# Order of row tiles in the combination of an attention kernel, and the queue of its first feature loads

## The chip, the cores and the metric

The program runs on one core of one Trainium2 chip. The metric is the device time of one execution in microseconds (us). The engines are TensorE (PE, matrix products; PEld is its weight load), VectorE (DVE), ScalarE (ACT), GpSimd (POOL) and SyncE (SP), which here only issues DMAs. Each engine works through its own instructions in the order of the program, and semaphores hold one back until the results that it needs are there.

## What is computed

The reference has two independent halves, laid side by side in the output. Half B is a two-dimensional Fourier transform, a product with a complex weight, and the inverse; the change doesn't touch it. Half A is attention with a memory, 32 heads of 18 columns, over 2048 rows in four groups of 512:

```python
for s in range(N):                       # N = 4 groups of L = 512 rows
    qs, ks, vs = q[:, :, s], k[:, :, s], v[:, :, s]
    p = softmax(qs @ ks.T * scale + mask)      # causal mask
    a_dot = p @ vs
    pq = phi(qs)                         # features
    a_mem = (pq @ M) / (pq . z + 1e-6)
    outs.append(g * a_mem + (1 - g) * a_dot)
    M = M + phi(ks).T @ vs;  z = z + sum(phi(ks))
return o @ wo
```

## The kernel before

The 576 columns of half A (32 heads x 18) lie on partitions, as five row tiles: t = 0 to 3 have 126 rows (seven heads), the fifth, t = 4, has 72, which the kernel lays out as 96 by repeating 24 rows (`host_wo`, `atables`). Products in 32 bits are split in a high and a low part, so that three products of parts stand for one.

`attention` (L959) is a loop of 133 steps t; step t treats one head of one group (32 steps to a group). In a step, `s1` finds the row maxima of the scores for the head ten steps ahead (PE L660 to L669, DVE L664 and L670), `s2` makes the scores again, transposed, and their exponentials (PE L703, L707, L712; ACT L704, L709, L713; causal selections on POOL), and `pv` mixes the values (PE L733). `mpath` (L678) brings the maxima of four heads into two rows of Q: casts on POOL (L685), a transposition on PE (L689), a copy on ACT and a small DMA on POOL's queue (L693). The loads of the stacks Q and K are put in a list `q` and issued by SP, two to a step.

Beside this run two kinds of other work. `lane` holds generators that are taken one piece further in each step. `bg` is a list of generators of which `run_bg` takes one piece at fixed places: in the middle and at the end of every second step, and now and then at the end of the others. So the order of everything on each engine is written out by the program; nothing is planned at run time. `later(1, f)` (L924) runs f at the end of the step in which it is called from `run_bg`. `s.now` is the number of the step that ended last.

The background work of group g, from its step 11 or so on:

- `ux_load` (L824) loads the unnormalized attention result of the group before, tile by tile, into three buffers. For t = 4 it is one DMA with a first dimension of 2 and a second of 48 rows (L829), for the others one of 126 rows (L826).
- `combine(g-1)` (L834) works through five tiles. For a tile, PE spreads the reciprocal denominators over rows (`pb`, L854), DVE multiplies (L859; L857 for the first group) and POOL or, from `now` = 117 on, DVE adds the memory's part (L860). Two tiles later ACT makes the high part `oh` (L848) and POOL or DVE the low part `ol` (L843). For t = 4, `tail` (L830) copies 32 rows of the high part into the last rows of `oh` and `ol`: on ACT, or on DVE when `now` is over 116.
- `mem1(g, t)` (L810) multiplies the features `pq` of a tile by the memory (PE L814), copies (ACT L816), spreads and multiplies by its denominators (PE L820, DVE L821). It also has the next group's features loaded (`pq_load`, L774).
- `oproj` (L879) is the output projection: four blocks of 128 rows in two halves; a half is 14 products of parts on PE (L891) with a pause after the seventh, and a copy on ACT (L893).
- `mixed(g)` (L864) strings these together by letters: c is a piece of `combine(g-1)`, m a piece of `mem1`, p a piece of `oproj(2)`, in the last group only. In the first groups `between` does the projection afterwards.

PSUM banks for `pb`, `pn` and `po` come from `bank` (L807): one buffer "post" while `now` < 119, then three buffers "s1" until 130, then "s2", which also holds the scores of `s2`. So until then a `pb` has to wait until the `pb` or `pn` before it has been read.

After step 132 a loop takes the rest of `bg` piece by piece. In its rounds 3, 5 and 7 stands `last_tile` (L896), which combines a tile of the fourth group (PE L901, DVE L902 and L903, ACT L904, DVE L909); then `last_proj` (L917) makes the last output products (L923).

The features of the second group, `pq_load(1, .)`, are loaded at steps 16 to 20 through SP's queue (L989).

Of the kernel before, what the change touches and what calls it, by code (L numbers as in the profile page):

```python
# [393 lines left out]
class ATT:  # L394
# [356 lines left out]
    def recip(s,src,dst,gate,eps,load,slack=0):  # L751
# [21 lines left out]
        yield  # L773
    def pq_load(s,g,t):  # L774

        r=126 if t<4 else 72
        x=s.tp.tile([126,512],F32,name="pq",bufs=5)
        s.nc.sync.dma_start(x[:r],s.pqD[g][126*t:126*t+r])
        s.pq[g,t]=x
# [19 lines left out]
    def between(s,g,lane):  # L799

        o=s.oproj(g-1)
        for _ in range(4):
            next(o)
            yield
        yield from s.den(g+1,lane)
        yield from o
    def bank(s,name,r=126):  # L807

        return (s.ps if s.now<119 or s.now>130 else s.ps1).tile([r,512],F32,name=name,tag="post" if s.now<119 else "s1" if s.now<131 else "s2")
    def mem1(s,g,t):  # L810
        nc=s.nc; r=126 if t<4 else 96; e=126 if t<4 else 72
        pn=s.bank("pn")
        M=s.Mst[g][:e,t,:r]
        nc.tensor.matmul(pn[:r],M,s.pq.pop((g,t))[:e],start=True,stop=True)  # L814
        am=s.tp.tile([126,512],F32,name="am",bufs=5)
        nc.scalar.copy(am[:r],pn[:r])  # L816
        if g<3: s.later(1,lambda: s.pq_load(g+1,t))
        yield
        pb=s.bank("pb")
        nc.tensor.matmul(pb[:r],s.sel[:,t,:r],s.rc["rd"],start=True,stop=True)  # L820
        nc.vector.tensor_tensor(am[:r],am[:r],pb[:r],op=OP.mult)  # L821
        s.am[t]=am; s.amg[t]=g
        yield
# [10 lines left out]
    def combine(s,g):  # L834
# [6 lines left out]
        def low(u):  # L841
            r=126 if u<4 else 96
            eng().tensor_tensor(s.ol[u][:r],s.am[u][:r],s.oh[u][:r].bitcast(F32),op=OP.subtract)  # L843
        for t in range(7):
            if t>1:
                u=t-2; r=126 if u<4 else 96
                s.oh[u]=tp.tile([128,512],F32R,name="oh",bufs=5); s.ol[u]=tp.tile([128,512],F32R,name="ol",bufs=5)
                nc.scalar.copy(s.oh[u][:r],s.am[u][:r])  # L848
                if u==4: s.later(1,lambda oh=s.oh[4],ol=s.ol[4]: s.tail(oh,ol)) if s.now<117 else s.tail(s.oh[4],s.ol[4])
                if s.now<117: low(u)  # L850
            if t<5:
                r=126 if t<4 else 96; x=xs[t]
                pb=s.bank("pb")
# [4 lines left out]
                else:  # L858
                    nc.vector.tensor_tensor(x[:r],x[:r],pb[:r],op=OP.mult)  # L859
                    eng().tensor_tensor(s.am[t][:r],x[:r],s.am[t][:r],op=OP.add)  # L860
                if t<2: s.later(1,lambda t=t: s.ux_load(g,t+3))
            if t>1 and s.now>=117: low(t-2)
            yield
    def mixed(s,g):  # L864

        c=s.combine(g-1); M=[s.mem1(g,u) for u in range(5)]
        P=s.oproj(2) if g==3 else None
        for x in "cccccm"+"cmmcmmcmmcmm"+"m" if g<3 else "c"*9+"p"*8+"mp"*8:
            if x=="c": next(c,None); yield
            elif x=="p": next(P); yield  # L870
            else:
                while M:
                    try: next(M[0]); break
                    except StopIteration: M.pop(0)
                yield
# [3 lines left out]
    def oproj(s,g):  # L879
        nc=s.nc  # L880
        oh,ol=s.oh,s.ol
        for tb in range(4):
            ob=s.tp.tile([128,576],F32,name="ob")
            c=slice(128*tb,128*tb+128)
            for hf in range(2):
                ps=s.bank("po",128)[:,:288]
                w=slice(288*hf,288*hf+288)
                L=[(a,b,t) for a,b in ((oh,s.woh),(oh,s.wol),(ol,s.woh)) for t in range(4)]+[(oh,s.woh,4),(ol,s.wol,4)]
                for i,(a,b,t) in enumerate(L):
# [69 lines left out]
    def attention(s,tp,ps):  # L959
# [20 lines left out]
        for t in range(133):  # L980
# [7 lines left out]
            st=t%32  # L988
            if 16<=t<21: s.pq_load(1,t-16)  # L989
            if t==34: bg.append(s.den(1,lane))  # L990
            if st==8 and g>0:
                def ln(g=g):
                    r=s.recip(s.rD[g-1],s.rrD[g-1],s.g1,False,"rr",2)
                    for i in range(8):
                        next(r)
                        if 2<i<6: s.ux_load(g-1,i-3)
                        yield
# [180 lines left out]
```

## Time and profile before

| | us |
|---|---|
| median of 3 runs | 720.09 (719.54 to 721.27) |
| profiled execution | 716.54 |
| its span, first to last instruction | 714.8 |
| ACT busy | 448.5 |
| POOL busy | 213.0 |
| DMA queue of SP, share of 16 engines' span | 50.9% |

The profile is of one execution. Its page gives busy times and a chain of waits; the trace behind it can be asked for single stretches: a timeline by engine (start, duration, engine, line, operation, and in brackets the idle time ahead of it and what ended that), the chain in order of time, waits by line, and tables of busy time, granted PE clock and DMA share in chosen windows. Times in it count from the span's start. The busy time of PE is modelled and overlaps from one product to the next, so that a product's length in a run of them is read from start to start.

### The profile page before, as it was taken

What the parts mean: (1) busy time and instruction counts of PE and PEld (TensorE: products, weight loads), DVE (VectorE), ACT (ScalarE), POOL (GpSimd) and SP (SyncE); (2) the same over time, 40 slices, a digit from 0 to 9 for tenths busy, and PEclk for the clock granted to TensorE, in tenths of its full rate; (3) what the DMA queues carried; (4) which work ended last, traced back from release to release, by engine and by line L of the source; (5) the groups of instructions that cost most, each with busy time, mean ns of one, the idle gap of its engine ahead of it and who ended that gap; (6) DMA issues with size and microseconds to landing.
All of it is one profiled execution on the core that took longest, in us unless ns stands there. A gap on an engine that the chain in (4) does not pass through costs nothing.

```text
span 714.8 us, 14142 instructions
## 1 busy us (share of the span) xinstructions
PE 674.9 (94%) x4835; PEld 494.8 (69%) x4835; DVE 554.4 (78%) x1231; ACT 448.5 (63%) x1006; POOL 213.0 (30%) x421
## 2 busy tenths in 40 slices
PE   4999999999999999999999899999999999997997
PEld 4999769879879779999844444444566445663676
DVE  6999989799799699787587778887667876577153
ACT  3667785575575564444487777777667676677631
POOL 2110000200200211465167433554233752336110
PEclk9999999999999999999999999999999999999999
DMA  9876436545373568899537665666656666441332
GB/s 343 266 233 204 149 123 199 184 157 185 136 232 127 165 208 270 213 230 233 169 108 183 170 170 145 176 165 167 152 126 178 163 167 152 101 137 45 99 93 77
DMA packets 83752, 121.56 MB, mean 170 GB/s; under 512 B 11498, under 2 KB 51032, under 8 KB 83544
## 3 DMA queue, kind: packets, MB, share of 16 engines
q1 hardware_dynamic: 77088, 104.62, 50.9%
q0 software_dynamic: 6592, 16.04, 8.1%
q8 instruction: 38, 0.62, 0.4%
q14 instruction: 34, 0.28, 0.1%
HBM read 82.30 MB, written 38.24 MB: 169 GB/s over the span
## 4 chain that ended last, share of the span: by engine, by line
PE 68%; DVE 14%; ACT 6%; DMA 5%; issue 5%; POOL 1%; SPq 0%; DVEq 0%; ACTq 0%; POOLq 0%
PE pv L733 10%; PE pjv L468 8%; PE pj L468 7%; PE po L891 6%; PE s L660 5%; PE i L300 4%; PE i L311 4%; PE s L668 4%; PE s L703 3%; DVE junk L664 3%; PE s L707 2%; PE po L923 2%; DVE pj L487 2%; PE c L163 2%; PE f L142 2%
## 5 line engine op out<-in xcount | busy, mean ns | idle before, releaser
L664 DVE CUSTOM_DVE_ANT_0 junk<-s,mask 128x512 bf16<-128x512 f32 (+1 forms) x256 | 141.6, 553 | 56.9 <-PE s L660 45.9
L670 DVE TENSOR_REDUCE mx<-s 128x4 f32<-128x512 f32 x128 | 87.9, 687 | 17.1 <-PE s L669 15.5
L704 ACT ACTIVATE P<-s 128x512 f32<-128x512 f32 x128 | 77.1, 602 | 21.1 <-PE s L703 18.5
L733 PE MATMUL pv<-P,vs 128*32 128x512 f32 (+3 forms) x1024 | 82.9, 443 | 0.0
L709 ACT ACTIVATE P<-s 128x512 f32<-128x512 f32 x128 | 77.0, 602 | 7.3 <-PE s L708 3.8
L713 ACT ACTIVATE P<-s 128x256 f32<-128x256 f32 x128 | 49.5, 387 | 49.6 <-PE s L712 49.6
L716 POOL TENSOR_SCALAR_AFFINE_SELECT P<-P 128x512 f32<-128x512 f32 x116 | 69.3, 635 | 4.9 <-ACT P L704 4.7
L733 PEld LDWEIGHTS pv<-P,vs 128*32 128x32 f32 x1024 | 27.0, 109 | 45.2 <-issue 43.1
L468 PE MATMUL pj<-x,wqkh 128*128 128x512 f32 x162 | 55.9, 406 | 0.0
L517 POOL MEMSET vt<- 128x32 f32 x16 | 2.4, 160 | 150.2 <-PE pm L527 122.8
L210 DVE TENSOR_TENSOR t<-Z 128x580 f32<-128x580 f32 x64 | 46.1, 755 | 0.1
L210 DVE TENSOR_TENSOR Z<-t 128x580 f32<-128x580 f32 x64 | 45.8, 755 | 0.1
L660 PE MATMUL s<-Ks,Qs 108*128 108x512 bf16 (+1 forms) x128 | 42.2, 329 | 0.0
L142 PE MATMUL f<-ftab,eh 128*128 128x290 f32 (+1 forms) x160 | 31.4, 315 | 9.5 <-DMA ftab<-ftab 9.5
L491 ACT CAST sp<-pj 128x512 bf16<-128x512 f32 x36 | 21.0, 585 | 30.0 <-DVE pj L487 30.0
L300 PE MATMUL i<-civ,Y 128*128 128x256 f32 (+1 forms) x288 | 37.9, 284 | 1.3 <-DVE T L332 1.3
L300 PEld LDWEIGHTS i<-civ,Y 128*128 128x128 f32 (+1 forms) x288 | 35.9, 181 | 1.6 <-DVE T L332 1.6
L311 PE MATMUL i<-itab,T 128*128 128x290 f32 (+1 forms) x224 | 36.1, 310 | 0.1
L468 PEld LDWEIGHTS pj<-x,wqkh 128*128 128x128 f32 x162 | 30.4, 188 | 7.7 <-issue 1.0
L468 PE MATMUL pj<-x,wqkl 128*128 128x512 f32 x90 | 35.5, 395 | 0.0
L468 PE MATMUL pj<-xh,wqkh 128*128 128x512 f32 x90 | 35.5, 395 | 0.0
L468 PE MATMUL pj<-xh,wqkl 128*128 128x512 f32 x90 | 35.5, 395 | 0.0
(226 smaller groups left out, 1836.4 us busy)
## 6 DMA issues: line engine op xcount, KB each, us to landing
qkD<-sp SPq DMA_DIRECT2D x36, 384.0 KB
Ks<-qkD SPq DMA_DIRECT2D x72, 144.0 KB
x<-qkD SPq DMA_DIRECT2D x60, 144.0 KB
Qs<-qkD SPq DMA_DIRECT2D x60, 144.0 KB
xin<-xb SPq DMA_DIRECT2D x16, 384.0 KB
cfw<-cfw POOLq DMA_DIRECT2D x16, 384.0 KB, 4.5
civ<-civ POOLq DMA_DIRECT2D x16, 384.0 KB, 7.4
vs<-vD SPq DMA_DIRECT2D x16, 330.0 KB
```

The costliest lines, as they stand in the source:

```text
L210: v.tensor_tensor(o,a,b,op=op)
L300: nc.tensor.matmul(p[:m,k],Y[i][:,q,c*128:c*128+m],cc[:,hl,o:o+256],start=n==0,stop=n==5)
L311: nc.tensor.matmul(p,x,t,start=n==0,stop=n==6)
L468: s.nc.tensor.matmul(out,a,b,start=i==0,stop=i==len(L)-1)
L660: nc.tensor.matmul(out,Q[:108,h,128*i:128*i+128],K[:108,h,:128*(i+1)],start=True,stop=True)
L664: nc.vector.tensor_tensor_reduce(out=junk[:,:w],in0=src,in1=s.mask[:,512-w:],scale=1.0,scalar=-3.0e38, op0=OP.add,op1=OP.max,accum_out=s.m ...
L670: nc.vector.tensor_reduce(out=s.mx[k][:,hh],in_=pa.rearrange("p (b c) -> p b c",c=128),axis=mybir.AxisListType.X,op=OP.max)
L704: nc.scalar.activation(P[0][:,hh],p0,AF.Exp,scale=SC)
L709: nc.scalar.activation(P[1][:,hh],p1,AF.Exp,scale=SC)
L713: nc.scalar.activation(P[2][:,hh],p2,AF.Exp,scale=SC)
L716: if k<29: nc.gpsimd.affine_select(out=x,in_=x,pattern=pat+[[1,128]],compare_op=OP.is_ge,fill=0.0,base=0,channel_multiplier=-1)
L733: nc.tensor.matmul(s.pvt[32*hh:32*hh+32,128*j:],vt[:,j,19*h:19*h+32],mv[0][:,hh,mv[1]],start=j==0,stop=j==2,skip_group_check=True)
```

## The change

Four things are changed. The fifth row tile comes first: `ORD=(4,0,1,2,3)` is the order of the loads of `ux` and of the features, of `combine`, and of `mem1` in the first groups; the features of the fourth group are loaded so that its `mem1` keeps the order 0 to 4. In `combine` of the third group the high and low parts of a tile come three tiles later instead of two (`lag`), so that it has one piece more, which `mixed(3)` places behind the first piece of `oproj(2)`. In `oproj` the 14 products of a half go tile by tile: tile 4's high product, the high and low weights' products of tiles 0 to 3, tile 4's low product, then the low parts of tiles 0 to 3. The first features are loaded through POOL's queue.

```diff
--- before.py
+++ after.py
@@ -771,11 +771,11 @@
         nc.sync.dma_start(r,dst)
         s.rc[load]=r
         yield
-    def pq_load(s,g,t):
+    def pq_load(s,g,t,eng=None):
 
         r=126 if t<4 else 72
         x=s.tp.tile([126,512],F32,name="pq",bufs=5)
-        s.nc.sync.dma_start(x[:r],s.pqD[g][126*t:126*t+r])
+        (eng or s.nc.sync).dma_start(x[:r],s.pqD[g][126*t:126*t+r])
         s.pq[g,t]=x
     def den(s,g,lane):
         nc=s.nc; tp=s.tp
@@ -804,6 +804,7 @@
             yield
         yield from s.den(g+1,lane)
         yield from o
+    ORD=(4,0,1,2,3)
     def bank(s,name,r=126):
 
         return (s.ps if s.now<119 or s.now>130 else s.ps1).tile([r,512],F32,name=name,tag="post" if s.now<119 else "s1" if s.now<131 else "s2")
@@ -814,7 +815,7 @@
         nc.tensor.matmul(pn[:r],M,s.pq.pop((g,t))[:e],start=True,stop=True)
         am=s.tp.tile([126,512],F32,name="am",bufs=5)
         nc.scalar.copy(am[:r],pn[:r])
-        if g<3: s.later(1,lambda: s.pq_load(g+1,t))
+        if g<3: s.later(1,lambda: s.pq_load(g+1,t if g<2 else s.ORD.index(t)))
         yield
         pb=s.bank("pb")
         nc.tensor.matmul(pb[:r],s.sel[:,t,:r],s.rc["rd"],start=True,stop=True)
@@ -841,15 +842,16 @@
         def low(u):
             r=126 if u<4 else 96
             eng().tensor_tensor(s.ol[u][:r],s.am[u][:r],s.oh[u][:r].bitcast(F32),op=OP.subtract)
-        for t in range(7):
-            if t>1:
-                u=t-2; r=126 if u<4 else 96
+        lag=2 if g<2 else 3
+        for p in range(5+lag):
+            if p>=lag:
+                u=s.ORD[p-lag]; r=126 if u<4 else 96
                 s.oh[u]=tp.tile([128,512],F32R,name="oh",bufs=5); s.ol[u]=tp.tile([128,512],F32R,name="ol",bufs=5)
                 nc.scalar.copy(s.oh[u][:r],s.am[u][:r])
                 if u==4: s.later(1,lambda oh=s.oh[4],ol=s.ol[4]: s.tail(oh,ol)) if s.now<117 else s.tail(s.oh[4],s.ol[4])
                 if s.now<117: low(u)
-            if t<5:
-                r=126 if t<4 else 96; x=xs[t]
+            if p<5:
+                t=s.ORD[p]; r=126 if t<4 else 96; x=xs[t]
                 pb=s.bank("pb")
                 nc.tensor.matmul(pb[:r],s.sel[:,t,:r],s.rc["rr"],start=True,stop=True)
                 if g==0:
@@ -858,14 +860,14 @@
                 else:
                     nc.vector.tensor_tensor(x[:r],x[:r],pb[:r],op=OP.mult)
                     eng().tensor_tensor(s.am[t][:r],x[:r],s.am[t][:r],op=OP.add)
-                if t<2: s.later(1,lambda t=t: s.ux_load(g,t+3))
-            if t>1 and s.now>=117: low(t-2)
+                if p<2: s.later(1,lambda p=p: s.ux_load(g,s.ORD[p+3]))
+            if p>=lag and s.now>=117: low(u)
             yield
     def mixed(s,g):
 
-        c=s.combine(g-1); M=[s.mem1(g,u) for u in range(5)]
+        c=s.combine(g-1); M=[s.mem1(g,u) for u in (s.ORD if g<3 else range(5))]
         P=s.oproj(2) if g==3 else None
-        for x in "cccccm"+"cmmcmmcmmcmm"+"m" if g<3 else "c"*9+"p"*8+"mp"*8:
+        for x in "cccccm"+"cmmcmmcmmcmm"+"m" if g<3 else "c"*9+"p"+"c"+"p"*7+"mp"*8:
             if x=="c": next(c,None); yield
             elif x=="p": next(P); yield
             else:
@@ -885,7 +887,7 @@
             for hf in range(2):
                 ps=s.bank("po",128)[:,:288]
                 w=slice(288*hf,288*hf+288)
-                L=[(a,b,t) for a,b in ((oh,s.woh),(oh,s.wol),(ol,s.woh)) for t in range(4)]+[(oh,s.woh,4),(ol,s.wol,4)]
+                L=[(oh,s.woh,4)]+[(oh,b,t) for t in range(4) for b in (s.woh,s.wol)]+[(ol,s.wol,4)]+[(ol,s.woh,t) for t in range(4)]
                 for i,(a,b,t) in enumerate(L):
                     r=126 if t<4 else 128
                     nc.tensor.matmul(ps,a[t][:r,c],b[:r,t,w],start=i==0,stop=i==13)
@@ -986,14 +988,14 @@
                 if 0<n<13: q+=s.stack_dmas(n+3,1)
                 if n+2<16: q.append(lambda n=n: s.load_v(n+2))
             st=t%32
-            if 16<=t<21: s.pq_load(1,t-16)
+            if 16<=t<21: s.pq_load(1,s.ORD[t-16],nc.gpsimd)
             if t==34: bg.append(s.den(1,lane))
             if st==8 and g>0:
                 def ln(g=g):
                     r=s.recip(s.rD[g-1],s.rrD[g-1],s.g1,False,"rr",2)
                     for i in range(8):
                         next(r)
-                        if 2<i<6: s.ux_load(g-1,i-3)
+                        if 2<i<6: s.ux_load(g-1,s.ORD[i-3])
                         yield
                     yield from r
                     bg.append(s.mixed(g))
```

## The prediction

> **What bounds the kernel now.** I read the busy shares first, then the chain of work that ended last, then the waits, and at last single stretches by engine. The page's first part gives the owner of the span:
>
> ```profile
> PE 674.9 (94%) x4835; PEld 494.8 (69%) x4835; DVE 554.4 (78%) x1231; ACT 448.5 (63%) x1006; POOL 213.0 (30%) x421
> ```
>
> TensorE (PE) is busy 94% of 714.8 us, and the change takes no matrix product away. So it can only win back PE's idle time, some 40 us in many pieces, at the few places that it touches. The largest such place is in the third group, where the chain of waits leaves PE:
>
> ```profile
> 650.52 6.94 DMA ux<-uD
> ...
> 657.55 0.70 DVE ux L859
> ...
> 658.26 0.70 DVE am L860
> ...
> 659.01 0.50 issue
> 659.51 0.59 ACT P L709
> ...
> 660.15 0.32 PE s L707
> ```
>
> Columns: start, duration, what. Row tile 4 is loaded last, with the two-part transfer of L829. It lands 6.94 us after its issue begins. VectorE (DVE) stands before its product L859 until then; ScalarE (ACT) stands before tile 4's high part with the exponential L709 queued behind; and PE needs the bank that L709 frees. The PE rows of that stretch, and the clock in stretches of 3.41 us (busy time of PE, PEld, DVE, ACT, POOL, then clock, DMA share, GB/s), show the price:
>
> ```profile
> 660.15 0.32 PE L707 MATMUL s<-x,Ks 110*128 110x384 bf16 x1 [2.02 <-ACT P L709]
> ...
> 665.82 0.39 PE L703 MATMUL s<-x,Ks 110*128 110x512 bf16 x1
> ```
> ```profile
> 8.73:12.14 3.41, 2.03 (x7) 1.55 (x7) 2.39 (x5) 0.83 (x1) 0.00 (x0) 1.00 1.14 390
> ...
> 657.26:660.67 3.41, 1.40 (x11) 0.78 (x15) 3.09 (x5) 1.98 (x5) 0.27 (x1) 1.00 0.03 10
> 660.67:664.08 3.41, 3.41 (x22) 1.77 (x15) 1.62 (x4) 1.64 (x4) 0.00 (x0) 0.50 0.00 0
> 708.46:711.87 3.41, 1.49 (x12) 1.25 (x10) 1.77 (x4) 1.45 (x4) 0.00 (x0) 1.00 0.58 220
> 711.87:714.80 2.93, 0.00 (x0) 0.00 (x0) 0.00 (x0) 0.00 (x0) 0.00 (x0) 0.50 0.41 147
> ```
>
> PE idles 2.02 us, and then runs 3.41 us at half clock, which costs 3.41 x 0.5 = 1.7 us more. Two stretches with about 2 us idle (3.41 - 1.40 and 3.41 - 1.49) are followed by half clock, and one with 1.38 us idle (3.41 - 2.03) isn't. From 665.82 on, PE has a backlog of output products until the tail.
>
> **The change, part by part.** Times are of the profiled execution (716.54 us, of which 714.8 are its span); I carry the difference over to the median of the runs shown, 720.09, which lies 3.55 above it.
>
> *First features by GpSimd's queue.* These rows are SP's queue, GpSimd (POOL) and PE around steps 16 to 22:
>
> ```profile
> 391.08 1.98 SPq L644 DMA_DIRECT2D Qs<-qkD  x2
> ```
> ```profile
> 390.46 1.41 POOL L629 TENSOR_TENSOR woh<-woh,wol 128x576 fp32r<-128x576 f32 x1
> 392.10 0.20 POOL L685 CAST mh<-mg 128x16 bf16<-128x16 f32 x1 [0.23 <-PE s L703]
> ...
> 394.73 0.67 POOL L693 DMA_DIRECT2D x<-mts  x1
> ```
> ```profile
> 393.29 0.32 PE L668 MATMUL s<-Ks,x 108*128 108x384 bf16 x1 [0.39 <-DVE mg L664]
> ```
> ```profile
> 401.23 0.38 PE L668 MATMUL s<-x,Qs 108*128 108x384 bf16 x2 [1.02 <-DMA pq<-pqD]
> ```
> ```profile
> SPq L644 <- DMA pq<-pqD: 7.2, 8, 1.4
> ```
>
> Five loads leave SP's queue, three of them ahead of the last pieces of the Qs stack, issued from 391.08 on, which the product at 401.23 reads first. SP itself stood 7.2 us, 8 times, behind earlier feature loads (0.9 each). Three loads fewer bring the last piece forward by up to 3 x 0.9 = 2.7 us, more than PE's stall of 1.02 us: take -1.0, with 0 as the other end. On POOL two issues of about 0.67 us (the row of L693) now stand between L629, which ends at 391.87, and the casts for the maxima at 392.10. These start at 391.87 + 1.34 = 393.2, 1.1 us late, and PE's transposition behind them with them. PE's next product waited 0.39 us for DVE anyway, so about +0.6. The later issues fall ahead of causal selections whose readers come a us or more after them. Sum **-0.4**, ends -1.0 and +1.1.
>
> The Trainium skill, "Trainium Kernel Development and Optimization", section "Key Constraints", speaks against this part: transfers from all queues share the same 16 engines, and another issuer saves only the sequencer's issue time. By it the -1.0 would be 0 and the part +0.6. SP's 7.2 us of waiting for the features' landings above disagrees in part, so I keep it as a rival.
>
> *Order 4, 0, 1, 2, 3 in the first two groups.* The instructions are the same; tile 4's two copies of L833, some 0.6 us each on ACT by L848's row further down, come some steps sooner, where ACT waits for PE between exponentials, and leave a place like it. Take 0, ends -0.6 and +0.6: one copy in PE's way or out of it. The products tile by tile are the same 14 per half block, seven ahead of the pause and seven behind it, at the same cost: 0.
>
> *Third group.* With two tiles loaded last that have 126 rows, the stall on L829's transfer goes: the load of the fourth, in SP's row below, began at 648.99 and its reader at 652.37 on DVE did not wait, so such a load takes at most 3.4 us. What is late next is found in the rows of DVE, PE, ACT, and of L833 by its source line:
>
> ```profile
> 648.99 0.33 SPq L826 DMA_DIRECT2D ux<-uD  x1
> ```
> ```profile
> 652.37 0.68 DVE L859 TENSOR_TENSOR ux<-ux,pb 126x512 f32<-126x512 f32 x1
> 653.08 0.69 DVE L860 TENSOR_TENSOR am<-ux,am 126x512 f32<-126x512 f32 x1
> ```
> ```profile
> 652.26 0.27 PE L712 MATMUL s<-Qs,Ks 110*128 110x256 bf16 x1
> 653.17 0.23 PE L689 MATMUL mt<-idb,mh 128*128 128x128 bf16 x1 [0.63 <-POOL mh L686]
> 653.24 0.38 PE L854 MATMUL pb<-rr,sel 96*96 96x512 bf16 x1
> 653.46 0.38 PE L703 MATMUL s<-Qs,Ks 110*128 110x512 bf16 x1
> ```
> ```profile
> 652.66 0.62 ACT L848 CAST oh<-am 126x512 fp32r<-126x512 f32 x1
> 653.17 0.61 ACT L709 ACTIVATE P<-s 128x512 f32<-128x512 f32 x1
> ```
> ```profile
> L833 DVE CAST oh<-oh x1: 420/420/420, 660.8 to 660.8; 32x512 fp32r<-32x512 f32 x1
> ```
>
> In the old order the product of the fourth tile runs on DVE at 652.37 and frees the only "post" bank at 653.05, before PE asks for it. In the new order the step of the fourth tile (p = 3, now = 117) first makes tile 4's high part on ACT, which ends at 652.66 + 0.62 = 653.28, and puts the two copies of `tail` on DVE behind it, 0.42 each, 0.45 from start to start: DVE waits for ACT, and L859 starts at 653.33 + 0.90 = 654.23, ends at 654.91. The next `pb` on PE waits for that bank, and behind it stand the scores of the next step: 653.24 becomes 654.95, **+1.7 us of a new wait**. After that ACT sets the pace: with PE 1.7 us late, the exponentials and three high parts (0.5 us from start to start) run end to end from 657.2, and L709 of step 120 ends at about 660.05, so PE's L707 stands at 660.2, where it stood before. The idle time is then in pieces, 0.5 + 1.7 around 653 and 0.4 + 0.7 in the first output products, about 1.1 in each stretch of 3.41 us, so the clock stays whole. Step 121's mixing, which ran at half clock, runs at the full one. The second half of the first output block now waits for tile 3's high part, which step 122 makes behind its first exponential: some 0.9 us. The L703 of step 123, at 665.82 before, then comes at 664.35, but one half of seven output products, 0.93 us, has been put off by the added step "c". Equal work stands at 664.35 + 0.93 = 665.28: **-0.5**, and without the clock's 1.7 us in the old run it would be +1.1.
>
> *The shifted step in the tail.* The string of mixed(3) is one step longer, so one half product comes behind the first last_tile instead of ahead of it. There the chain is DVE's:
>
> ```profile
> 673.32 0.93 PE po L891 x7
> ...
> 685.70 0.86 PE pn L814 x2
> ...
> 687.48 0.23 PE pb L901
> ...
> 692.38 0.70 DVE ux L903
> ...
> 693.10 0.62 ACT P L904
> ...
> 694.07 0.38 PE pb L820
> ```
>
> From 687.48 to 694.07, 6.59 us, the order of DVE's work sets the end, through L903 and ACT. PE's work in it is 3 half products of 0.93, 2 of L814 of 0.86 and 5 `pb` of 0.23, 5.66 us, so 0.93 us is free. One more half product just fits in: the last_tile starts 0.93 sooner and the stretch keeps its length: **-0.9**, ends -0.9 and 0.
>
> Sum: -0.4 + 0 - 0.5 - 0.9 = **-1.8 us**: 716.54 becomes 714.7, and at the median 720.09 - 1.8 = **718.3 us**.
>
> **The rivals.**
>
> *The wait goes and nothing replaces it.* If tile 4's high part is ready sooner than I work out, or PE has slack behind the bank, the new 1.7 us falls away: -1.8 - 1.7 = -3.5, so 716.6. For it: DVE has no maxima left to find after step 117. Against it: L848 sits behind an exponential of its own step on ACT, which nothing in the change brings forward.
>
> *The half clock stays.* The idle pieces of 0.5 and 1.7 us lie within 2.4 us. If one stretch takes in both, PE runs the next at half clock: -1.8 + 1.7 = -0.1, so 720.0. Where the stretches begin in a given execution decides. The Trainium skill, "TensorE: Matmul & The Clock Gate", section "What's actually happening", has a free-running window of about 3.4 us, which the steps of the rows bear out; it asks for an idle window, and here 2.0 us idle were enough.
>
> *SP gains nothing.* The Qs stack lands as late as before: -1.8 + 1.0 = -0.8, so 719.3.
>
> *Slower: the maxima queue behind the features.* On POOL's queue the small transfer of L693 now follows four loads. The rows of the large load on that queue, of that transfer, and its reader:
>
> ```profile
> itab<-itab POOLq DMA_DIRECT2D x1, 1160.0 KB, 9.2
> ...
> x<-mts POOLq DMA_DIRECT2D x12, 8.0 KB, 6.4
> ```
> ```profile
> 405.97 0.38 PE L703 MATMUL s<-x,Ks 110*128 110x512 bf16 x1
> ```
>
> Four loads, 144 + 3 x 252 = 900 KB, take 900/1160 x 9.2 = 7.1 us with that rate and 14 at half of it, beside SP's traffic; begun at 391.9 they end at 399 to 406. The maxima, issued about 2 us late at 396.9, land 6.4 later at 403.3 in the good case, and at 406 + 6.4 = 412.4 in the bad one, where PE waits 412.4 - 406.0 = 6.4 us: -1.8 + 6.4 = +4.6, so 724.7. It decides from 406.0 on.
>
> **How the numbers follow.** My forecast, with small changes around it, has 0.35; the wait that isn't replaced 0.30, the half clock 0.12, SP without gain 0.10, the slower rival 0.13. A measurement of this kernel tells about 0.3% from no change, 2.2 us, so "same" is 717.9 to 722.3. Of the forecast's 0.35 I put a quarter below 717.9, since it lies 0.4 above it: faster 0.30 + 0.09 = 0.39; same 0.26 + 0.12 + 0.10 = 0.48; slower 0.13. The range leaves out the outer parts: from 715.0, below the first rival by the rest of the feature part's good end and of the orders', to 722.3, where half the slower rival lies beyond.
>
> **What would show it.** In the profile after: no wait of L859 for a load in the third group; two L833 copies on DVE ahead of the third L859 there, a wait of DVE for L848 and of PE's L854 for L859 of 1 to 2 us; PE's L707 two steps on within 1 us of 660; a full clock to the end of the last product; no wait of L668 for a load near 401, and a later L689 near 393; last_tile's first product about 1.5 us sooner, against L703 of step 123. I am wrong if the bank's wait is missing, if PE waits near 406, or if the first two groups move by more than 1 us.

## The result, and the profile after

The changed kernel takes **723.37 us**, the median of four runs (723.18 to 723.44), beside 719.82 us (719.35 to 721.27) for four runs of the kernel before on the same chip. The ratio is 1.0046, with a 95% interval from 1.0028 to 1.0063: slower by 0.46%. The forecast was 718.3, and the range ended at 722.3.

The profiled execution of the changed kernel took 723.4 us, with a span of 721.7. That of the kernel before was quicker than its own median by 3.3 us, so the two profiles lie 6.9 us apart where the medians lie 3.55 apart. I read the profiles for places, and the repeated runs for sizes. In the runs further down, two executions, one of run 9 (1095.93 us) and one of the kernel before beside it (1295.36 us), were far slower at a lower clock and are left out of ratios and clocks.

The first part of the page after. PE has the same products, and is busy 2.1 us longer:

```profile
PE 677.0 (94%) x4835; PEld 495.2 (69%) x4835; DVE 556.1 (77%) x1232; ACT 449.9 (62%) x1006; POOL 216.3 (30%) x425
```

To find where 6.9 us went, I set the start of L703 in each step t beside that of the kernel before. The lag is +0.4 us up to step 18 (ahead of everything that the change touches), then it moves in few places:

| step | lag after it, us | moved by | forecast for it |
|---|---|---|---|
| 19 | +0.8 | +0.35 | +0.6 |
| 22 | -0.4 | -1.2 | -1.0 |
| 24 and 25 | +2.6 | +3.0 | 0 |
| 52 to 54 | +5.8 | +3.3 | 0 |
| 62 and 65 | +5.0 | -0.8 | 0 |
| 88 and 89 | +6.5 | +1.5 | 0 |
| 119 to 123 | +6.9 | +0.35 | -1.5 |
| end of the span | +6.9 | 0 | 0 (the half product owed fits in) |

**Steps 19 to 25.** Three views of the profile after: POOL's timeline (start, duration, engine, line), the chain of waits, and PE's row. (Lines of the changed kernel and of the runs are shifted by one to three: `pb` is L856 or L857 for L854, the product with it L861 or L862 for L859.)

```profile
392.26 1.18 POOL L778 DMA_DIRECT2D pq<-pqD  x2
393.44 0.21 POOL L685 CAST mh<-mg 128x16 bf16<-128x16 f32 x1
...
395.90 0.53 POOL L778 DMA_DIRECT2D pq<-pqD  x1
396.43 0.66 POOL L693 DMA_DIRECT2D x<-mts  x1
```
```profile
396.43 7.88 DMA x<-mts
...
404.40 0.26 ACT mts L692
...
404.71 0.38 PE s L660
```
```profile
404.71 0.38 PE L660 MATMUL s<-x,Qs 108*128 108x512 bf16 x1 [1.31 <-ACT mts L692]
```

The casts at 393.44 stand behind two issues, as forecast, and the wait of L668 near 401 is gone. But the small transfer of L693, 8 KB, which was issued at 396.43 behind four feature loads, takes 7.88 us. Nobody waits for what it brings. The next copy L692 writes the buffer that it reads, the only one of that name (L691, `bufs=1`), so ACT waits at 404.40, with the exponentials behind it, and PE stands for 1.31 us.

The same transfer was slow in the kernel before too, with no feature load ahead of it on POOL's queue, but there L692 came later. L693's transfer of 394.73 by its tile, and ACT's row, both before:

```profile
L693 POOL DMA_DIRECT2D x<-mts x1: 666/666/666, 394.7 to 394.7; - x1
...
DMA to landing us min/median/max: 7.1/7.1/7.1
```
```profile
403.21 0.25 ACT L692 COPY mts<-mt 32x128 bf16<-32x128 bf16 x1
```

It landed at 401.8, 1.4 us ahead of L692. Counted from the L703 of step 19, the issue comes 0.9 us later in the profile after, the transfer takes 0.8 us longer, and L692 is ready 1.1 us sooner, because the wait of L668 is gone. So 1.4 us to spare became 1.5 us of waiting, and the gain at L668 is itself part of the reason.

**The clock.** The windows of 3.41 us of the profile after (busy time of PE, PEld, DVE, ACT, POOL, then clock, DMA share, GB/s), at this place and in the third group:

```profile
402.15:405.56 3.41, 1.76 (x13) 0.78 (x16) 2.05 (x6) 1.73 (x6) 0.60 (x1) 1.00 0.67 187
405.56:408.97 3.41, 3.41 (x23) 1.43 (x16) 1.11 (x5) 1.24 (x3) 2.45 (x5) 0.50 0.78 186
658.15:661.56 3.41, 1.24 (x9) 0.64 (x7) 2.34 (x9) 2.88 (x8) 0.80 (x4) 1.00 0.41 143
661.56:664.97 3.41, 3.41 (x20) 0.90 (x18) 3.38 (x5) 1.08 (x2) 1.95 (x3) 0.50 0.03 5
```

I set the windows so that the stretches at clock 0.50 fill one each. The stretch ahead of them, in which PE idles 1.65 us (3.41 - 1.76) or 2.17 us (3.41 - 1.24), decided: behind it PE does in 3.41 us the work of 1.7. So L692's wait, 1.31 us of PE's time, costs 3.0 in the table.

**Steps 52 to 54.** Rows of SP and PE in the profile after, then SP's row of the kernel before, then SP's waits in the profile after from 440 to 470 (total, times, longest, in us):

```profile
446.56 0.68 SPq L830 DMA_DIRECT2D ux<-uD  x1
...
468.39 0.31 SPq L771 DMA_DIRECT2D rr<-rrD  x1
```
```profile
470.74 0.38 PE L856 MATMUL pb<-rr,sel 96*96 96x512 bf16 x1 [1.49 <-DMA rr<-rrD]
...
477.46 0.38 PE L668 MATMUL s<-x,Qs 108*128 108x384 bf16 x2 [1.48 <-DMA uD<-U]
```
```profile
462.35 0.31 SPq L771 DMA_DIRECT2D rr<-rrD  x1
```
```profile
SPq L749 <- DMA ux<-uD: 2.2, 1, 2.2
```

The load of the reciprocals `rr` is issued 6.04 us later than before, at a place where the whole run is only 2.6 us late. Tile 4's slow transfer (L830, formerly L829) now comes first, and SP itself stands 2.2 us in front of a store (L749) until it has landed. What SP issues behind it comes late: `rr`, on which the first `pb` waits 1.49 us, and, as I read it, the stack pieces for L668 in step 54 (the row names a store of U that L668 doesn't read, but which stands in the same queue). Of step 88's +1.5 us I have no run of its own; DVE waited there for a load of `ux`:

```profile
572.14 0.69 DVE L861 TENSOR_TENSOR ux<-ux,pb 126x512 f32<-126x512 f32 x1 [1.71 <-DMA ux<-uD]
```

In the runs below, steps 88 and 89 lose 0.4 to 1.5 us in all four executions with tile 4 early in one transfer (with such a wait in three of them), and nothing in the four with tile 4 early in two halves.

**Third group.** DVE's and PE's rows after, then the L703 of step 123 after, which stood at 665.82 before:

```profile
659.81 0.42 DVE L834 CAST oh<-oh 32x512 fp32r<-32x512 f32 x1 [0.85 <-ACT oh L850]
660.24 0.42 DVE L834 CAST ol<-oh 32x512 fp32r<-32x512 f32 x1
660.69 0.69 DVE L861 TENSOR_TENSOR ux<-ux,pb 126x512 f32<-126x512 f32 x1
```
```profile
661.43 0.50 PE L856 MATMUL pb<-rr,sel 96*126 96x512 bf16 x1 [1.53 <-DVE ux L861]
...
672.68 0.39 PE L703 MATMUL s<-x,Ks 110*128 110x512 bf16 x1
```

The stall on the load is gone, and the new wait stands where the prediction put it: two copies of `tail` on DVE behind ACT's high part, and `pb` 1.53 us behind them (forecast 1.7). The idle pieces fell into one stretch of 3.41 us, and the half clock stayed (the last window above).

### The profile page after: what moved, and what is told of

Same layout as the page of the kernel before. It is cut to its first block, busy times and chain, and to the rows that moved or that the text cites. A ratio compares the mean times of both kernels' runs of the same rounds, so it can differ in the third digit from the quotient of the medians.

```text
span 721.7 us, 14141 instructions
## 1 busy us (share of the span) xinstructions
PE 677.0 (94%) x4835; PEld 495.2 (69%) x4835; DVE 556.1 (77%) x1232; ACT 449.9 (62%) x1006; POOL 216.3 (30%) x425
## 4 chain that ended last, share of the span: by engine, by line
PE 62%; DVE 14%; DMA 9%; ACT 7%; issue 5%; POOL 2%; SPq 1%; DVEq 0%; ACTq 0%; POOLq 0%
PE pv L733 8%; PE pj L468 7%; PE pjv L468 6%; PE po L893 6%; PE s L660 4%; PE i L300 4%; PE i L311 4%; PE s L668 3%; PE s L703 3%; DVE junk L664 2%; PE po L925 2%; PE s L707 2%; DVE pj L487 2%; DMA xin<-xb 2%; PE c L163 2%
## 5 line engine op out<-in xcount | busy, mean ns | idle before, releaser
L893 PE MATMUL po<-woh,oh 126*128 126x288 f32 (+1 forms) x120 | 37.0, 352 | 1.5 <-ACT oh L850 1.5
```

The lines of the kernel that those rows point to most:

```text
L893: nc.tensor.matmul(ps,a[t][:r,c],b[:r,t,w],start=i==0,stop=i==13)
```

## The experiments

The theory: three waits, each with a half clock that may follow it. (1) L692 waits for the single `mts` buffer behind POOL's queue. (2) SP's queue is held by tile 4's two-part transfer, moved early. (3) `pb` waits for DVE, which waits for ACT. The rivals are beside each run. The ratio is to the kernel before, run alongside on the same chip; the clock is the mean granted over the runs compared, and 0.001 of it is at most 0.72 us, where PE has work all the time. Runs 1 to 4 were made on one chip, 5 to 12 on a second and 13 to 16 on a third, so that runs of different rows are compared by their ratios.

| run | what | median, us | ratio (95%) | clock |
|---|---|---|---|---|
| 1 | features by POOL only | 721.80 | 1.0049 (1.0028 to 1.0069) | 0.9942 |
| 2 | the same, four row ranges for `mts` | 719.01 | 1.0003 (0.9982 to 1.0024) | 0.9977 |
| 3 | first two groups' order only | 719.40 | 1.0025 (1.0003 to 1.0048) | 0.9953 |
| 4 | third group (and products) only | 720.02 | 1.0021 (0.9995 to 1.0048) | 0.9956 |
| 5 | run 3, tile 4's load split | 715.07 | 0.9942 (0.9921 to 0.9962) | 0.9987 |
| 6 | before, tile 4's load split | 713.87 | 0.9932 (0.9905 to 0.9958) | 0.9992 |
| 7 | changed kernel, four row ranges | 721.27 | 1.0028 (1.0006 to 1.0050) | 0.9952 |
| 8 | before, features three steps later | 718.57 | 1.0004 (0.9980 to 1.0027) | 0.9970 |
| 9 | run 6 with the third group | 716.57 | 0.9971 (0.9947 to 0.9994) | 0.9974 |
| 10 | run 9, `tail` behind the product | 714.20 | 0.9949 (0.9928 to 0.9969) | 0.9988 |
| 11 | run 6, features by POOL | 718.00 | 0.9993 (0.9974 to 1.0013) | 0.9955 |
| 12 | changed kernel, all three mended | 714.42 | 0.9933 (0.9905 to 0.9961) | 0.9995 |
| 13 | run 11, four row ranges | 715.70 | 0.9968 (0.9948 to 0.9989) | 0.9981 |
| 14 | run 12 without the `tail` part | 716.88 | 0.9977 (0.9959 to 0.9996) | 0.9973 |
| 15 | run 12 without the row ranges | 717.56 | 0.9989 (0.9973 to 1.0004) | 0.9965 |
| 16 | run 12 without the split | 718.33 | 0.9997 (0.9976 to 1.0019) | 0.9969 |

The kernel before ranged from 714.76 to 722.28 us in the 35 runs beside runs 1 to 4, with a mean clock of 0.9971. In run 1 the lower clock makes at most (0.9971 - 0.9942) x 720 = 2.1 us of the 3.5 lost. By the runs of the kernel before, which took 3.2 us more at a clock of 0.994 than at 1.000 (last section), it makes some 1.5.

### The feature loads: runs 1, 2, 7, 8, 11, 13

Run 1 is the kernel before with this:

```diff
-    def pq_load(s,g,t):
+    def pq_load(s,g,t,eng=None):
-        s.nc.sync.dma_start(x[:r],s.pqD[g][126*t:126*t+r])
+        (eng or s.nc.sync).dma_start(x[:r],s.pqD[g][126*t:126*t+r])
-            if 16<=t<21: s.pq_load(1,t-16)
+            if 16<=t<21: s.pq_load(1,t-16,nc.gpsimd)
```

> Only the first feature loads go to POOL's queue; all orders are as before. Theory A (the small maxima transfer L693 finishes late behind the loads and the copy L692 into its single buffer waits for it): L692 near 404 waits 1 to 2 us for a DMA, PE's L660 behind it 1 us, then one stretch of 3.41 us at half clock; the wait of L668 near 401 is gone. Lag at step 24 about +2 us against the kernel before, and the time about 722. Theory B (my forecast on record): -0.4 us, 719.6. Theory C (the 2 us in the trace of after are chance of where the clock's stretches begin): no wait of L692, time within 1 us of before.

Run 2 adds, in `mpath`:

```diff
-        mt=s.sm.tile([32,128],BF,name="mts",bufs=1)
+        s.mtb=s.mtb if k else s.sm.tile([128,128],BF,name="mts",bufs=1); mt=s.mtb[32*(k%4):32*(k%4)+32]
```

> As the run before, but the copies L692 go to four row ranges of one tile in turn, so that none waits for the transfer of the one before. Theory A: the wait of L692 and the half clock behind it are gone, what stays is -1.2 us (no wait for the features) and +0.4 (casts behind two issues): about 719.3. Rival (the transfers are late whatever the buffer, and their readers or the 16 engines set the time): as slow as the run before, 722, with PE waiting at 406 or later for the maxima themselves.

Run 1 cost 0.49%, as much as the whole change, and run 2 took it back. But the profiled execution of run 1 loses its time elsewhere than theory A said. PE's rows and SP's in run 1:

```profile
404.81 0.59 PE L668 MATMUL s<-x,Qs 108*128 108x384 bf16 x2 [3.25 <-DMA Qs<-qkD]
```
```profile
388.06 3.15 SPq L644 DMA_DIRECT2D Qs<-qkD  x6
```

SP had issued all six Qs pieces by 391.21, and PE still waited for them until 404.81; with PE so late, L692 found its buffer free. From 396 to 400 the DMA share was 1.02, beside 0.65 in the kernel before and 0.82 in the changed kernel; which loads were in the way of the Qs pieces is not shown. It fits what the Trainium skill says in "Trainium Kernel Development and Optimization", section "Key Constraints": the queues share the 16 engines. Over the profiles, L668 waited at this place in all seven executions with the loads on SP at steps 16 to 20 (0.35 to 2.16 us), and in two of ten with POOL (3.25 and 1.30). So the gain of 1.0 us was there, though not reliably. In runs 4 and 9, with the loads on SP and waits of 1.93 and 2.16 us, a half clock followed this wait too.

Run 11 puts run 1's change on the kernel with the split load (run 6 below), whose time varies less.

> Kernel before with the split load of tile 4, and the first feature loads on POOL's queue with the single buffer of the maxima. Theory A (waits for the maxima's transfer, L692 near 404 or the Qs pieces at step 22, with a half clock behind them): 2 to 3.5 us above the split alone, ratio 0.996 to 0.998. Rival (POOL's queue is neutral, and what the run of POOL alone lost was chance of the clock): 0.9932.

ACT's and PE's rows of run 11, the wait in full size, and ACT's row of run 12, with row ranges:

```profile
406.19 0.26 ACT L692 COPY mts<-mt 32x128 bf16<-32x128 bf16 x1 [3.25 <-DMA x<-mts]
```
```profile
406.50 0.38 PE L660 MATMUL s<-x,Qs 108*128 108x512 bf16 x1 [3.08 <-ACT mts L692]
```
```profile
402.01 0.25 ACT L692 COPY mts<-mt 32x128 bf16<-32x128 bf16 x1
```

0.9993 against 0.9932 is 0.61%, 4.4 us. Run 13 adds the row ranges to run 11:

> Kernel before with the split load of tile 4, the first features by POOL's queue, and four row ranges in turn for the maxima's copy. Theory A (the single buffer is the whole price of POOL's queue): as the split alone, ratio 0.992 to 0.995, no wait of L692 for a DMA. Rival (the queue costs more than the buffer: casts behind two issues, other transfers late): 0.996 to 0.999, as with the single buffer (0.9993).

It came out at 0.9968, between runs 6 and 11 and in the range of the rival: L692 waits no more, but PE's L703 of step 24 waits 0.34 us for the maxima themselves, the reader that my slower rival had named:

```profile
404.95 0.39 PE L703 MATMUL s<-x,Ks 110*128 110x512 bf16 x1 [0.34 <-DMA x<-mts]
```

Whether POOL's queue has a price of its own beside the buffer stays open: run 13 lies 0.36% above run 6, and run 12, which has the same loads, on it; the intervals are some 0.2 to 0.3% to each side. Run 7 is the changed kernel with the row ranges alone.

> The changed kernel with four row ranges of one tile in turn for the copy L692, nothing else. Theory A (the wait for the maxima's transfer and the half clock behind it are worth about 2.7 us): 2 to 3 us below the changed kernel, a ratio to before of 1.001 to 1.002, no wait of L692 for a DMA. Rival (the loss of the first part sits in what the engines carry, not in the buffer): ratio 1.0046 as the changed kernel.

1.0028 against 1.0046, with overlapping intervals: the right direction, not settled by itself. Run 8 moves the loads instead (`19<=t<24` and `t-19` in place of 16, through SP, in the kernel before).

> The kernel before with the five feature loads at steps 19 to 23 instead of 16 to 20, through SP as before, so that they stand behind the Qs pieces of this stretch. Theory A (the features compete with the Qs pieces that step 22 reads first, in whichever queue they stand): L668 near 401 doesn't wait, nor a half clock behind it, and the mean lies 1 to 2.5 us below before, with less spread. Rival (SP's issue order there costs nothing but the 1.02 us seen once): at most -1 us; and if the later loads hit the Ks pieces or the reciprocal, a wait near steps 30 to 34.

The wait of L668 near 401 went, as theory A had it, but the time is that of before (1.0004). With that wait gone, L692 waited 0.42 us for L693's transfer here too, with no feature load on POOL's queue. A wait like L668's stood 17 us later, for the Ks pieces:

```profile
418.72 0.38 PE L668 MATMUL s<-Ks,Qs 108*128 108x384 bf16 x2 [1.38 <-DMA Ks<-qkD]
```

So the load on the engines moves on, and moving the features in SP's queue is worth nothing that can be measured.

### The first two groups' order, and tile 4's load: runs 3, 5, 6

Run 3 is the changed kernel with the features through SP, the old list of products and lag 2, and `ORD` only in the first two mixed groups (the second line wherever `ORD` stands in `combine` and for `ux_load`):

```diff
+    def o(s,g): return s.ORD if g<2 else range(5)
...
-                u=s.ORD[p-lag]; r=126 if u<4 else 96
+                u=s.o(g)[p-lag]; r=126 if u<4 else 96
```

Runs 5 and 6 split the load in `ux_load`, run 6 in the kernel before:

```diff
-            s.nc.sync.dma_start(s.ux[t][:96],bass.AP(tensor=a.tensor,offset=a.offset,ap=[[24*512,2],[512,48],[1,512]]))
+            [s.nc.sync.dma_start(s.ux[t][48*i:48*i+48],bass.AP(tensor=a.tensor,offset=a.offset+24*512*i,ap=[[512,48],[1,512]])) for i in range(2)]
```

> Only the order 4, 0, 1, 2, 3 in the first two mixed groups; features by SP, third group and products as before. Theory A (the two-part load of tile 4, now early, holds up SP's queue, and the reciprocal's transfers and the stacks behind it come late): PE's pb of the first mixed group waits 1 to 2 us for the load of rr near 470, lags of +1.6 at steps 52 and 54 and +1.5 at step 88, in sum about +4 us in the profile: 722 to 724. Theory B (my forecast): 0 with ends of 0.6: 720. Rival C (the lags at 52 to 88 in after are a consequence of the earlier delay at step 24, which shifts this stretch against SP's queue): no lag here without the POOL part, 720.

> As the run with only the first two groups' order, but tile 4's load is two transfers of 48 rows instead of one of 2 x 48. Theory A (the slow two-part transfer, now early, holds SP's queue): tile 4 lands within 4 us of its issue, SP issues the load of rr 1 to 2 us ahead of step 51's L703 as in the kernel before, PE's wait of 1.5 to 2.7 us for rr goes, and the time is that of before within 0.15%. Rival (the order itself, with loads of ux bunched where the reciprocal's transfers stand, or chance): rr still 1.5 us behind step 51 and the time 0.25% above before.

PE's row and SP's wait in run 3, then PE's row in run 5:

```profile
469.27 0.59 PE L857 MATMUL pb<-rr,sel 96*96 96x512 bf16 x1 [2.65 <-DMA rr<-rrD]
```
```profile
SPq L749 <- DMA ux<-uD: 3.8, 1, 3.8
```
```profile
468.81 0.38 PE L857 MATMUL pb<-rr,sel 96*96 96x512 bf16 x1
```

With the one slow transfer early, SP stood 3.8 us and PE 2.65 us; with the same order and the load in halves, neither did. Over the profiles, the first `pb` waited for `rr` in all four executions that have tile 4 early in one transfer (the changed kernel 1.49, run 3 2.65, run 7 2.37, run 16 1.61 us), and in none of the four with tile 4 early in halves (runs 5, 12, 14, 15). In the old order with one transfer it waited in run 2 (1.29 us), and not in the kernel before or runs 1, 4 and 8. So it stands near its limit in the old order too. The order alone is not the cost: run 5 lies 0.10% above run 6, within the intervals. It is 0.58% quicker than the kernel before, where I had expected the same time within 0.15%: the halves pay in the third group as well, as run 6 shows.

> The kernel before with tile 4's load as two transfers of 48 rows. Theory A (the stall of the third group is the length of the two-part transfer, 6.94 us): each half lands in 3 to 4 us, DVE's wait in the third group shrinks from 6.9 to about 4 us, PE's 2.02 us of idle time and the half clock go where they occur: -1 to -3 us. Rival (the landing time is that of the engines' load, not of the pattern): no change, within 0.1%.

Run 6 takes 0.68% off the kernel before, 4.9 us, where I had expected 1 to 3. Its rows of SP and DVE in the third group:

```profile
650.83 0.77 SPq L829 DMA_DIRECT2D ux<-uD  x2
```
```profile
653.95 0.69 DVE L843 TENSOR_TENSOR ol<-am,oh 126x512 fp32r<-126x512 f32 x1
654.55 0.68 DVE L859 TENSOR_TENSOR ux<-ux,pb 96x512 f32<-96x512 f32 x1
```

DVE takes tile 4's product with no wait, 3.72 us after the issue of the two halves began, where 6.94 us passed before. The L703 of step 123 comes 3.2 us sooner against that of step 118: the 2.02 us of idle time, and the half clock of 1.7, less some 0.5 (0.46 of it a wait for ACT that stays). Another 0.7 us is won at step 62, where L668 waited 0.51 us in the kernel before; all 13 profiles with tile 4 early or in halves win it, and the four others beside the kernel before don't. The rest of the 4.9 us is not located. The Trainium skill, "DMA: Bandwidth & Descriptors", section "Why a DMA increments its semaphore by 16 and not by 1", has a rule that fits: a transfer goes to the largest number of engines, up to 16, that divides the slowest dimension of both sides; by it 2 x 48 rows go to two engines, 48 to sixteen. No row here shows the engines one by one, but 192 KB in 6.94 us beside 252 KB (126 rows) in at most 3.4 agree with it.

### The third group: runs 4, 9, 10, 14

Run 4 is the changed kernel with the features through SP and the same function `o` with `g==2` in place of `g<2`, so that `combine(2)` alone has the new order; lag 3, the shifted step and the products tile by tile stay. Run 9 is that with the split load, and run 10 moves `tail` in it:

```diff
-                if u==4: s.later(1,lambda oh=s.oh[4],ol=s.ol[4]: s.tail(oh,ol)) if s.now<117 else s.tail(s.oh[4],s.ol[4])
+                if u==4 and s.now<117: s.later(1,lambda oh=s.oh[4],ol=s.ol[4]: s.tail(oh,ol))
...
-            if p>=lag and s.now>=117: low(u)
+            if p>=lag and s.now>=117: low(u); u<4 or s.tail(s.oh[4],s.ol[4])
```

> Only the third group's order and lag 3 with the shifted step, and the products tile by tile; the rest as before. Theory A (new wait of pb for DVE, which waits for ACT's high part of tile 4, and with the idle pieces a stretch at half clock): a wait of L856 (or its like) for L861 of 1.5 us, half clock once near 655 to 660, lag against before unchanged within 0.5 us from step 118 to the end: 720.0. Theory B (my forecast for these parts, clock whole): -1.4 us: 718.7.

> Kernel before with tile 4's load as two of 48 rows, and on top the third group's new order, lag 3, the shifted step and the products tile by tile. The stall on the load is already gone by the split, so that only what the new order adds is left. Theory A (pb on PE waits 1.5 us for DVE, which waits for ACT's high part of tile 4 in front of the two copies): between step 118 and 123 1.7 to 2.0 us more than the split alone (-3.2 us against before), the wait of L857 for L862 in the trace, ratio to before about 0.9957, or 0.998 where the clock drops too. Rival (the new order costs nothing by itself, DVE has room): as the split alone, 0.9932.

> As the run before, but the two copies of tail stand on DVE behind that step's product with pb and behind its low part, not ahead of them. Theory A: the wait of PE's pb for DVE of 1.5 us goes, and the stretch from step 118 to 123 comes within 0.7 us of the split alone: ratio 0.993 to 0.9942. Rival (not the copies but ACT's three high parts at the pace of the exponentials set the stretch): as the run before, about 0.9957.

PE's row and two windows of run 4, the same of run 9, then DVE's and PE's rows of run 10:

```profile
661.19 0.38 PE L857 MATMUL pb<-rr,sel 96*126 96x512 bf16 x1 [1.53 <-DVE ux L862]
```
```profile
656.73:660.14 3.41, 2.30 (x24) 1.05 (x17) 2.41 (x9) 2.52 (x7) 1.69 (x3) 1.00 0.68 205
660.14:663.55 3.41, 2.36 (x23) 0.98 (x23) 3.31 (x6) 1.97 (x6) 1.17 (x2) 1.00 0.07 20
```
```profile
658.60 0.38 PE L857 MATMUL pb<-rr,sel 96*126 96x512 bf16 x1 [1.53 <-DVE ux L862]
```
```profile
655.90:659.31 3.41, 1.24 (x8) 0.52 (x6) 2.48 (x8) 2.53 (x8) 1.03 (x3) 1.00 0.34 125
659.31:662.72 3.41, 3.41 (x23) 1.17 (x22) 3.38 (x5) 1.66 (x4) 1.87 (x3) 0.50 0.02 3
```
```profile
652.69 0.68 DVE L862 TENSOR_TENSOR ux<-ux,pb 126x512 f32<-126x512 f32 x1
...
654.71 0.42 DVE L835 CAST oh<-oh 32x512 fp32r<-32x512 f32 x1
```
```profile
653.56 0.38 PE L857 MATMUL pb<-rr,sel 96*126 96x512 bf16 x1
```

The wait is 1.53 us in all five profiles with `tail` ahead of the product (the changed kernel, runs 4, 7, 9 and 14), and absent where it stands behind. A half clock followed it in three of the five: not in run 4 nor in run 14. In these two the idle time falls into two stretches, 1.05 to 1.11 us in each; in the three others 1.99 to 2.17 us fall into one. From step 118 to 123 runs 4 and 14 take 1.5 us more than run 10, which has no such wait, and the three with a half clock 2.3 to 3.1 more. In run 4 this stretch is 1.26 us shorter than before, where the prediction had 1.5. Against the split load alone, run 9 costs 0.39% and run 10 0.17%, and the L703 of step 123 gains 3.2 us from step 118 on in run 6, 2.8 in run 10 and 0.1 in run 9. So by the rows theory A holds and its rival falls; run 10's ratio, 0.9949, lies between what the two had, and its interval holds both. Run 4's own time, 1.0021 with an interval that holds 1, neither shows nor excludes the half clock by itself.

### The whole change, mended: runs 12, 15, 16

Run 12 is the changed kernel with the three edits shown: split load, four row ranges, `tail` behind the product. Runs 14, 15 and 16 leave one out.

> The changed kernel, with the split load of tile 4, four row ranges in turn for the maxima's copy, and the two copies of tail behind DVE's product. If the three named causes are all of it: 1 us either side of the split alone, ratio 0.992 to 0.9945. If something of the change that was not named costs time: above 0.996.

> The changed kernel with the split load and the four row ranges, but the two copies of tail where the change has them. If the wait of pb behind them is the third group's price in the whole change as it was alone: 2 to 3 us above the fully mended kernel (0.9933), ratio 0.996 to 0.998, and a wait of L856 for L861 of 1.5 us. Rival (in the whole change the wait falls into other idle time): 0.993 to 0.995.

> The changed kernel with the split load and the moved copies of tail, but the single buffer of the maxima. If the buffer's wait holds in the whole change: 3 to 4.5 us above the fully mended kernel, ratio 0.997 to 1.000, with a wait of L692 of 1 to 3.5 us. Rival: 0.993 to 0.995.

> The changed kernel with the four row ranges and the moved copies of tail, but tile 4's load as one transfer of 2 x 48 rows, early in the first two groups. The third group has this load early too, so that only the first groups pay: 2.5 to 5 us above the fully mended kernel, ratio 0.997 to 1.000, with a wait of PE's pb for rr of 1.5 to 2.7 us near 468. Rival: 0.993 to 0.995.

Each wait came back where its mend was left out. PE's row of run 14, ACT's of run 15, and PE's of run 16:

```profile
654.17 0.38 PE L856 MATMUL pb<-rr,sel 96*126 96x512 bf16 x1 [1.53 <-DVE ux L861]
```
```profile
405.97 0.25 ACT L692 COPY mts<-mt 32x128 bf16<-32x128 bf16 x1 [2.54 <-DMA x<-mts]
```
```profile
469.79 0.38 PE L856 MATMUL pb<-rr,sel 96*96 96x512 bf16 x1 [1.61 <-DMA rr<-rrD]
```

Above run 12 they cost 0.44% (third group), 0.56% (buffer) and 0.64% (load). These add up to 1.64%, more than the 1.13% between run 12 and the changed kernel, as runs 1, 3 and 4 alone add up to 0.95% where the whole lost 0.46%. With intervals of 0.2 to 0.3% on each ratio, I can't say how much of the excess is chance and how much is waits that overlap. Run 12 beats both kernels, and so does run 6, with one edit; between the two nothing can be told apart.

## Why the prediction was wrong

**First features by POOL's queue: wrong in sign. The step that failed is that I asked only who reads what L693 brings, and not who next writes its source.** I had -0.4 with ends -1.0 and +1.1; alone it measured +0.49%, 3.5 us. The gain of 1.0 at L668 and the delay of the casts were in the profile (-1.2 and +0.35). The slower rival had the queue, the transfer L693 and the loads ahead of it, but followed only the reader of its data, PE's L703 at 406.0. The first to wait was the next writer of its source, L692 on ACT, which comes earlier, and PE's scores behind it. I gave it 0.13 and a price of 6.4 us on another condition. Of the four profiles with these loads on POOL's queue and the single buffer, three have the wait of L692 (the changed kernel, runs 11 and 15); run 1's has 3.25 us at L668 in its place. In the trace of before this copy had 1.4 us to spare, and the part's own terms, a later issue and PE 1.0 us sooner, use that up. Two readings were off besides: the 6.4 us for the landing are a median over the execution, and this very transfer had taken 7.1; and the 7.2 us in which SP stood behind feature loads are those of the whole execution, of which 3.5, in three waits, belong to this place.

**Order 4, 0, 1, 2, 3 in the first two groups: "The instructions are the same", take 0.** This step failed too: I counted the two copies of `tail` and left out that the order moves L829's transfer to the head of SP's queue, though its 6.94 us stood in the first chain that I quoted. It measured +0.25% alone, and +3.3 and +1.5 us in the profile of the whole. With the load in halves the order costs nothing that can be measured, so the zero held for the instructions, and not for the transfer.

**Third group: the mechanism right, the clock wrong.** The stall on the load went, and the wait of `pb` came, 1.53 us for 1.7. L703 of step 123 gained 1.26 us in run 4, against 1.5. "So the clock stays whole" is what failed: I spread the idle time over two stretches of 3.41 us, about 1.1 in each, as it fell in runs 4 and 14, while in the execution after 2.17 us fell in one. Which of the two comes is luck, by where the stretches begin. I gave the half clock 0.12; it came in three profiles of five. My example of a stretch with 1.38 us idle and no half clock behind it was none: the trace's record of the clock begins at 15.55 us, and from 12 to 15 us PE's products of 290 columns stand 241 ns apart, beside some 135 ns from 15.6 on. PE ran at half speed there, though the row of 8.73 prints 1.00.

**Shifted step in the tail: right.** From step 123 to the end the changed kernel is neither quicker nor slower than before (lag 6.9 at both), though it had one half product more to do there. Against that L703 `last_tile`'s first product comes at 21.6 us, 21.5 before; the sign that had it 1.5 us sooner against it did not come, and by the sum itself the two move together.

**Products tile by tile: 0**, not run alone; run 12, which has them, lies 0.01% from run 6, which hasn't.

**What was there to be seen.** The largest gain stood in the first chain quoted: the two-part transfer. The change worked around it by putting it where it had longer to land, while one line that splits it is worth 0.68% in the old order.

## What to carry to other kernels

A transfer has two ends: follow who reads what it brings, and who next writes what it reads, above all where a buffer is the only one; and a gain elsewhere can bring that writer forward. A load that is moved ahead takes its length with it, so look at what stands behind it in its queue; a slow transfer is better made quick than early. And price a wait of 1.5 us on a busy TensorE with the clock: in the third group it was worth 1.5 us, or 2.3 to 3.1, by how it fell into the stretches of 3.41 us.

## What the runs showed of the hardware

- **The spread goes with the clock.** Of the 35 runs of the kernel before beside runs 1 to 4, the six at a mean clock of 1.000 took 716.6 us on average and the five at 0.994 took 719.8. The kernels without the long waits (runs 6 and 12, clock 0.9992 and 0.9995) stayed within 711.9 to 715.3. The Trainium skill, "TensorE: Matmul & The Clock Gate", section "What's actually happening", calls the window free-running, so that the moment of a change varies from run to run. The two stretches at half clock after begin 256.0 us apart, 75 times 3.41, and the same 1.53 us of wait with and without a half clock (runs 9 and 4) agree with that. The same section of the Trainium skill lets the clock fall after an idle window of about 3.4 us; here 1.65 us of idle time in one were enough.
- **How much idle time in one stretch.** I went through the stretches of 3.41 us of all 18 profiles, on the grid of each clock record, up to PE's last product; the busy time of PE is modelled. All 13 stretches at full clock with 1.65 us of idle time or more were followed by half clock, and none with 1.46 us or less. In between, 1.56 us (run 15) was, and 1.58 and 1.61 us (runs 7 and 16) were not.
- **The 8 KB of L693 had no fixed time to landing.** At this place it took 6.8 to 7.8 us in the eight profiles with the features on SP's queue, and 7.9 to 9.9 in the ten with them on POOL's, where four loads, 900 KB in all, stand ahead of it. The quickest of its 32 transfers in the kernel before took 2.0.
- **A free issuer is not a free engine.** With SP's six Qs pieces issued by 391.21, PE waited for them until 404.81, 13.6 us later, while POOL's loads were under way.
